# Q and K as token rows with DMA transposes, V once per token, one-bank PSUM tiles and a new written-out order in an adaLN block with dilated local attention and an MLP

## Chip, cores and metric

The kernel runs on one core of a Trainium2 chip. The metric is the device time in microseconds (us) of one execution; the median of several runs is given. A profiled execution has its own time, and the working below is made against that one.

## What is computed

One transformer block on 2048 tokens of width 448, in bf16. A conditioning vector `c` gives six modulation vectors (`sa, ca, ga, sb, cb, gb`). The first half is attention over a window of 8 keys at distance 2 (a token sees itself and the tokens 2, 4, ... 14 before it) with 16 heads of 28. The second half is an MLP of width 1792 with a layer norm of its own inside.

```python
mod = (_silu(c) @ w_mod).reshape(c.shape[0], 6, 1, -1)        # sa, ca, ga, sb, cb, gb
h = _layernorm(x) * (1 + ca) + sa
qkv = (h @ wqkv) ...                                          # q, k, v: 16 heads of 28
off = arange(8) * 2 ; idx = pos[:, None] - off[None, :]       # keys of a query
logits = einsum('bhsd,bhswd->bhsw', q, k[idx]) * 28 ** -0.5   # masked where idx < 0
o = einsum('bhsw,bhswd->bhsd', softmax(logits), v[idx])
x = x + ga * (o @ wo)
h = _layernorm(x) * (1 + cb) + sb
x = x + gb * (gelu(_layernorm(h) @ w1 + b1) @ w2 + b2)
```

## The kernel before

**Tiling.** Even and odd tokens never meet in the attention, so every buffer has a parity index `s` of two. A block `jb` (0 to 7) is 128 tokens of each parity, 256 in all. An attention step `i` (0 to 8) is 114 queries of each parity, two groups of 57, each with the 64 keys that it can see. A chunk `c` (0 to 3) of the MLP is two blocks, 512 tokens.

**Stages.** For a block: layer norm of `x` (`s1`, `r1`, `n1`: statistics, reciprocal root, normalising); the transposed block goes into `hT`, by TensorE and an eviction with the modulation (`tr`, `ev`, blocks 0 to 3) or by a DMA transpose with the modulation afterwards (`dT`, `sc`, blocks 4 to 7). Q and K come out of TensorE with their columns on the partitions (`qA`, `qB`: stationary `wqk`, a copy of the weights with heads padded to 32, made by `wc`; moving `hT`, 256 or 512 tokens), and one eviction by ScalarE per pair of banks (`qe`) puts them in `qT` and `kT`. V is computed for each step and not for each block, since the 64 keys of neighbouring groups overlap (`vA`, `vB`, lines 481 to 500, nine steps), and is evicted with keys on the partitions (`ve`).

An attention step is `L` (logits), `eA`, `eB` (exponential), `mA`, `mB` (mask), `AV` (sums, then the weighted values), `ln`, `rx` (reciprocal of the sum by logarithm and exponential), `mu` (division, into `qT`). Then for a block `wo` (output projection), `x1` (residual), `s2 r2 n2 h2 s3 r3 n3` (two layer norms and the modulation), `dY` (DMA transpose into `yT`). For an MLP chunk: `fA`, `fB` (seven pairs of 128 hidden columns), `ge` (gelu by ScalarE, 14), `f2` (second product, 14 matmuls for each of four groups of 128 tokens), `fo` (bias and residual) and `dS` (store).

A product with 448 inner elements is split over two row halves of TensorE that run side by side: part A is eight matmuls, part B six. Between them stands `ob`, an empty instruction on another engine's queue (line 437) that waits for part A and that part B waits for.

**What sets the order.** All instructions are written out by hand-made tables: `ORDER` is the sequence of items, and every engine gets its instructions in that sequence; `SLOTS` says which buffer each item uses. The four PSUM tiles of two banks each are `P`. SyncE (SP) issues all but one of the DMAs, in the same sequence, so a DMA behind a waiting one waits too; a DMA also waits for the eighth DMA before it. `tab` switches ScalarE between the table of exponential and logarithm and that of gelu, so the gelu of chunk 0 comes only after the steps that need the first table. `warm` are matmuls on zeros in the first microseconds.

Of the kernel before, what the change touches and what calls it, by code (L numbers as in the profile page):

```python
# [36 lines left out]
qA.0.1 ob.POOL.q.0.0 ob.ACT.q.1.2 n1.2 r1.3 qB.0.0 ob.ACT.q.0.1 qB.1.2 qe.0.0 tr.2 n1.3 qe.1.2 rowm ev.2.3 ev.2.2
ev.2.0 ev.2.1 tr.3 rowc qB.0.1 ev.3.2 ev.3.1 qA.0.2 ev.3.0 ev.3.3 s1.6 qA.1.1 ob.SP.q.0.2 qe.0.1 qB.0.2 ob.SP.q.1.1
qA.2.2 qe.0.2 dR s1.5 r1.6 qB.1.1 ob.SP.q.2.2 L.0 qe.1.1 s1.4 r1.5 qB.2.2 eA.0 dB qA.2.1 eB.0 mA.0 r1.4 qA.1.0 s1.7
ob.SP.q.2.1 qe.2.2 qB.2.1 ob.SP.q.1.0 qB.1.0 qe.2.1 qA.2.0 mB.0 r1.7 n1.4 dR2 qe.1.0 AV.0 ob.POOL.q.2.0 n1.5 dT.4  # L40
n1.6 qB.2.0 ln.0 qA.1.3 rx.0 dT.6 b1T ob.DVE.q.1.3 b1c qB.1.3 qe.2.0 mu.0 vA.1 dT.5 qe.1.3 vA.2 ob.POOL.v.1 wos vB.1
dW1.0.1 ob.ACT.v.2 n1.7 dW1.0.0 vB.2 ve.1 sc.4 L.1 dT.7 ve.2 qA.2.3 w2s.5 eA.1 rowf vA.3 ob.SP.q.2.3 eB.1 mA.1
qB.2.3 ob.SP.v.3 mB.1 vB.3 qe.2.3 sc.5 AV.1 ve.3 w2s.2 qA.3.3 sc.6 ln.1 qA.3.1 rx.1 ob.SP.q.3.3 sc.7 qB.3.3
ob.SP.q.3.1 mu.1 qB.3.1 qe.3.3 qA.4.3 w2s.0 qe.3.1 w2s.4 L.2 ob.SP.q.4.3 w2s.3 qB.4.3 eA.2 w2s.1 qA.4.0 w2s.6 qe.4.3
mA.2 wo.0 ob.SP.q.4.0 eB.2 mB.2 qB.4.0 x1.0 AV.2 qe.4.0 s2.0 xp.0 qA.3.2 ln.2 qA.4.2 rx.2 ob.SP.q.3.2 r2.0 qB.3.2
ob.ACT.q.4.2 mu.2 qB.4.2 qe.3.2 n2.0 L.3 qe.4.2 h2.0 wo.1 eA.3 s3.0 eB.3 qA.4.1 r3.0 qA.3.0 ob.ACT.q.4.1 n3.0 qB.4.1
ob.ACT.q.3.0 qB.3.0 mA.3 dY.0 qe.4.1 x1.1 vA.4 qe.3.0 vA.5 s2.1 ob.SP.v.4 xp.1 vB.4 ob.SP.v.5 L.4 ve.4 vB.5 mB.3
r2.1 eA.4 ve.5 mA.4 L.5 n2.1 eB.4 h2.1 eA.5 AV.3 mB.4 eB.5 vA.6 mA.5 ln.3 mB.5 ob.SP.v.6 s3.1 vB.6 rx.3 AV.4 ve.6
mu.3 r3.1 ln.4 vA.7 n3.1 rx.4 wo.2 ob.POOL.v.7 dY.1 mu.4 vB.7 x1.2 AV.5 ve.7 s2.2 xp.2 wo.3 ln.5 rx.5 fA.0.0 x1.3
tab.1 r2.2 fA.0.1 ob.SP.f.0.0 s2.3 fA.0.2 ob.SP.f.0.1 n2.2 r2.3 fB.0.1 ob.SP.f.0.2 mu.5 fB.0.2 ge.0.3 fB.0.0 ge.0.2  # L50
n2.3 fA.0.3 ge.0.4 h2.3 ge.0.0 fA.0.4 ob.SP.f.0.3 h2.2 ge.0.5 fB.0.3 ge.0.1 ob.SP.f.0.4 s3.3 fA.0.5 ge.0.7 ge.0.6
# [690 lines left out]
```

## Time and profile before

| | |
|---|---|
| median of 3 runs | 182.56 us (181.6 to 184.72) |
| profiled execution, span | 182.2 us |
| TensorE busy | 170.8 us (94% of the span), 2538 matmuls |
| VectorE, ScalarE, GpSimd busy | 112.5 us (62%), 105.0 us (58%), 43.3 us (24%) |
| mean granted TensorE clock | 0.958 of full speed |
| HBM read, written | 10.04 MB, 1.95 MB |

The profile shows the span from the first to the last instruction; no other time of that execution is recorded, so the span stands for it, and it lies 0.4 us below the median of the runs. Busy time of TensorE is the time in which a matmul was in the array or in its queue, so a stall behind a queued matmul can hide in it, and a half-speed clock makes the same matmuls look twice as busy. The granted clock is given for each stretch as a share of full speed.

### The profile page before, as it was taken

The page shows a single profiled execution, that of the slowest core. Times are in us where ns is not written, and L with a number is a line of the kernel's source. Part 1 is how long each engine was busy: PE and PEld are TensorE (multiplying, and loading weights), DVE is VectorE, ACT ScalarE, POOL GpSimd, SP SyncE. Part 2 cuts the span into 40 slices and gives each one's busy share as a digit, 9 for nine tenths or more (in the row PEclk, how much of TensorE's full clock was granted, in tenths as well). Part 3 has the DMA queues.
Part 4 walks back from the last instruction along what each step waited for, and adds up shares of the span by engine and source line. Part 5 has one row for each costly group of instructions (what it writes and reads, how often), then busy time and mean ns, then how long its engine had stood idle before and what let it go on. Part 6 is the DMA issues. An engine that isn't in the chain of part 4 may idle for free.

```text
span 182.2 us, 5815 instructions
## 1 busy us (share of the span) xinstructions
PE 170.8 (94%) x2538; PEld 86.3 (47%) x2539; DVE 112.5 (62%) x264; ACT 105.0 (58%) x145; POOL 43.3 (24%) x77
## 2 busy tenths in 40 slices
PE   7999679979999979999999999999999999999990
PEld 2556335634444453444454554554544554454550
DVE  5858757599969789589788604785970772002022
ACT  3177619777967497487884879650887000585000
POOL 7404062000050442062402500224520224400000
PEclk9969969999999995899999999999999999999998
DMA  5999994997000300300080130013103004100111
GB/s 150 321 393 302 375 312 101 117 255 153 4 4 2 61 4 4 63 0 5 0 105 14 56 58 4 4 24 84 54 4 58 0 0 108 54 0 0 54 50 50
DMA packets 21455, 15.51 MB, mean 85 GB/s; under 512 B 13301, under 2 KB 20982, under 8 KB 21430
## 3 DMA queue, kind: packets, MB, share of 16 engines
q1 hardware_dynamic: 21428, 15.14, 32.1%
q8 instruction: 20, 0.33, 0.8%
q14 instruction: 5, 0.04, 0.1%
q10 hardware_dynamic: 2, 0.00, 0.0%
HBM read 10.04 MB, written 1.95 MB: 66 GB/s over the span
## 4 chain that ended last, share of the span: by engine, by line
PE 74%; DMA 8%; DVE 7%; ACT 4%; issue 2%; SPq 1%; POOL 1%; DVEq 0%
PE P L660 21%; PE P L419 18%; PE P L428 13%; PE P L588 7%; PE P L489 7%; DMA rowd<-zt 3%; DMA bc<-rowd 3%; DMA yT<-in_w_mod_dram 2%; PE P L563 2%; DVE st L348 2%; PE P L522 1%; PE P L554 1%; PE P L261 1%; PE P L292 1%; ACT et L527 1%
## 5 line engine op out<-in xcount | busy, mean ns | idle before, releaser
L653 ACT ACTIVATE hm<-P,b1c 128x512 bf16<-128x512 f32 x56 | 34.1, 691 | 22.4 <-PE P L428 22.3
L660 PE MATMUL P<-w2s,hm 128*128 128x448 bf16 x224 | 43.4, 353 | 0.0
L660 PEld LDWEIGHTS <-hm 128*128 128x128 bf16 x224 | 21.6, 98 | 20.6 <-issue 0.8
L419 PE MATMUL P<-yT,w1s 64*128 64x512 bf16 x224 | 27.1, 376 | 0.2 <-DVE x L665 0.2
L597 POOL TENSOR_TENSOR xp<-x,gbb 128x896 f32<-128x896 bf16 x8 | 15.2, 1897 | 40.2 <-DVE x L593 27.7
L665 DVE TENSOR_TENSOR x<-P,xp 128x896 bf16<-128x896 f32 (+1 forms) x9 | 8.8, 985 | 25.8 <-PE P L660 25.7
L354 POOL TENSOR_SCALAR rs<-mv 128x2 f32<-128x2 f32 x22 | 6.7, 303 | 70.8 <-DVE mv L350 61.8
L428 PE MATMUL P<-yT,w1s 64*128 64x512 bf16 x168 | 20.9, 376 | 0.0
L348 DVE BATCH_NORM_STATS2 st<-x 128x6 f32<-128x448 bf16 x32 | 18.3, 615 | 0.9 <-DMA x<-in_A_x_dram 0.5
L489 PE MATMUL P<-wv,hT 64*64 64x448 bf16 x252 | 17.5, 397 | 0.4 <-SPq L437 0.2
L593 DVE TENSOR_TENSOR x<-P,x 128x896 bf16<-128x896 f32 x8 | 8.7, 1090 | 14.5 <-PE P L588 14.5
L419 PEld LDWEIGHTS <-w1s 64*128 64x128 bf16 x224 | 11.1, 94 | 13.0 <-issue 1.2
L527 ACT ACTIVATE et<-P 128x912 bf16<-128x912 f32 x18 | 16.1, 942 | 1.7 <-PE P L522 1.7
L419 PE MATMUL P<-hT,wqk 64*128 64x512 bf16 (+1 forms) x160 | 16.9, 347 | 0.1
L428 PE MATMUL P<-hT,wqk 64*128 64x512 bf16 (+1 forms) x120 | 13.6, 349 | 3.6 <-SPq L437 3.6
L355 POOL TENSOR_TENSOR rs<-rs,nhalf 128x2 f32<-128x2 f32 x22 | 16.0, 726 | 1.8
L568 ACT ACTIVATE rc<-P 128x912 f32<-128x912 f32 x9 | 8.5, 942 | 10.4 <-PE P L554 10.4
L540 DVE TENSOR_TENSOR et<-et,mask 128x912 bf16<-128x912 bf16 x18 | 11.3, 652 | 4.5 <-ACT et L527 4.4
L588 PE MATMUL P<-wo,qT 128*128 128x448 bf16 x64 | 13.5, 353 | 0.1
L428 PEld LDWEIGHTS <-w1s 64*128 64x128 bf16 x168 | 8.8, 94 | 9.4
L578 DVE TENSOR_TENSOR qT<-P,rc 128x456 bf16<-128x456 f32 x18 | 10.5, 624 | 2.9 <-ACT rc L573 2.9
L509 ACT CAST vs<-P 128x896 bf16<-128x896 f32 x9 | 8.1, 907 | 6.2 <-PE P L489 6.2
(79 smaller groups left out, 187.2 us busy)
## 6 DMA issues: line engine op xcount, KB each, us to landing
w1s<-in_B_w_dram SPq DMA_DIRECT2D x4, 448.0 KB, 11.7
w2s<-in_B_w_dram SPq DMA_DIRECT2D x2, 784.0 KB, 15.6
out_dram<-x SPq DMA_DIRECT2D x7, 224.0 KB, 2.3
hm<-in_w_mod_dram SPq DMA_DIRECT2D x1, 1344.0 KB
hm<-in_A_wqkv_dram SPq DMA_DIRECT2D x4, 224.0 KB, 5.1
x<-in_A_x_dram SPq DMA_DIRECT2D x1, 896.0 KB
yT<-in_w_mod_dram SPq DMA_DIRECT2D x3, 224.0 KB, 4.1
x<-in_A_x_dram SPq DMA_DIRECT2D x2, 224.0 KB
```

The lines of the kernel that those rows point to most:

```text
L348: nc.vector.bn_stats(out=self.st[:, b + s, :], in_=src[:, s, :])
L355: nc.gpsimd.tensor_tensor(out=r, in0=r, in1=self.nhalf[:], op=ALU.pow)
L419: mm = self.nc.tensor.matmul(outs[t], lhsT=lhs(t, r, kt), rhs=rhs(t, r, kt), start=(kt == 0), stop=False)
L428: mm = self.nc.tensor.matmul(outs[o], lhsT=lhs(o, r, kt), rhs=rhs(o, r, kt), start=False, stop=(n == 2))
L489: mm = self.nc.tensor.matmul(t[64 * s:64 * s + 64, o, 0:D], lhsT=self.hT[r, s, kt, k0:k0 + NK], rhs=self.wv[r, kt, :], start=(part == 0 an ...
L527: self.nc.scalar.activation(out=self.et[:, self.sl(f"e{i}"), 2 * h:2 * h + 2, :], in_=self.ps(f"L{'AB'[h]}{i}")[:, :, 0:8 * NQ], func=ACT.Exp,
L540: self.nc.vector.tensor_tensor(out=e, in0=e, in1=m, op=ALU.mult)
L578: self.nc.vector.tensor_tensor(out=self.qT[:, s, :, c0:c0 + SW], in0=self.ps(f"O{i}")[:, s, 0:8 * NQ].rearrange("p (m c) -> p m c", m=4), ...
L588: self.nc.tensor.matmul(p[:, s, 0:D], lhsT=self.qT[:, s, m, c0:c0 + 128], rhs=self.wo[:, m, :], start=(m == 0), stop=(m == 3))
L597: self.nc.gpsimd.tensor_tensor(out=self.xp[:, self.sl(f"xp{jb}"), :, :], in0=self.x[:, jb, :, :], in1=self.gbb2[:].unsqueeze(1).to_broadca ...
L653: self.nc.scalar.activation(out=self.hid(c)[:, ft, :], in_=self.ps(f"F{c}.{ft // 2}")[:, ft % 2, :], func=ACT.Gelu_apprx_tanh, bias=self.b ...
L660: self.nc.tensor.matmul(p[:, s, 0:D], lhsT=h[:, ft, 128 * b:128 * b + 128], rhs=self.w2s[:, ft, :], start=(ft == 0), stop=(ft == FT - 1))
```

## The change

**Q and K.** The operands change places: `hT` (128 tokens of a block and parity) is stationary and the weights move, 448 columns of Q and 448 of K. The result has tokens on the partitions. Two evictions (`qe`, one for Q and one for K, on ScalarE `A` or VectorE `D`) write it with heads padded to 32 into `qks`, and a DMA transpose (`qT`) of 128 rows by 1024 columns brings it into `qkT`, which takes the place of `qT` and `kT`. The padded copy of the weights (`wc`) goes.

**V.** It is computed once per block, evicted as two halves (`ve`), written to DRAM (`vw`, buffer `vd` with seven rows of zeros in front) and read back for each step and parity in the overlapping form (`vr`).

**PSUM.** Eight tiles of one bank. What was one instruction on two banks becomes two on one bank each: the exponential (`ex`, four a step), `ln`, `rx`, `mu`, `x1`, `fo`.

**Order.** Blocks 2 and 3 are transposed by DMA too (`NTR = 2`). The product for the modulation is cut into four parts that follow their loads (`mod`), `modc` sums them. `ORDER` and `SLOTS` are new throughout; the engine of each eviction stands in the item.

```diff
-i.ones i.z dX.0 dC i.one warm0 i.mask dM.0 dM.1 i.id dM.2 i.maskb i.maskc dM.3 i.eps i.pad dX.1 s1.0 cT warm1 dQ.0
+i.one i.mask i.qks i.z dM.0 dC cT silu0 i.maskc dX.1.1 dX.2.2 i.wo dO.1 dM.1 silu1 silu2 i.id s1.1 warm.0.5 dX.0.1
...
-        self.P = [ps.tile([128, 2, 512], FP32, name=f"P{i}") for i in range(4)]
+        self.P = [ps.tile([128, 512], FP32, name=f"P{i}") for i in range(8)]
...
-        def lhs(o, r, kt):
-            return self.wqk[r, kt, 128 * (2 * p + o):128 * (2 * p + o) + 128]
+    def qk(self, jb, s):
+        def lhs(o, r, kt):
+            return self.hT[r, s, kt, 128 * jb:128 * jb + 128]
         def rhs(o, r, kt):
-            return self.hT[r, :, kt, c0:c0 + 128 * nj]
+            return self.wqk[r, kt, D * o:D * o + D]
...
+    def qe(self, eng, jb, s, o):
+        out = self.qks[:, self.sl(f"q{jb}_{s}"), o, :].rearrange("p (h e) -> p h e", e=32)[:, :, 0:DH]
+        self.copy(eng, out, self.ps(f"Q{jb}_{s}")[o][:, 0:D].rearrange("p (h e) -> p h e", e=DH))
+
+    def qT(self, jb, s):
+        c0 = PADL + 128 * jb
+        src = self.qks[:, self.sl(f"q{jb}_{s}"), :, :].rearrange("p o n -> p (o n)")
+        self.nc.sync.dma_start_transpose(out=self.qkT[:, s, :, c0:c0 + 128], in_=src)
+
+    def v(self, jb):
+        def lhs(o, r, kt):
+            return self.hT[r, o, kt, 128 * jb:128 * jb + 128]
+
+        def rhs(o, r, kt):
+            return self.wv[r, kt, :]
...
+    def ve(self, eng, jb, s):
+        self.copy(eng, self.vst[:, self.sl(f"vw{jb}"), s, :], self.ps(f"V{jb}")[s][:, 0:D])
+
+    def vw(self, jb):
+        a = WIN - 1 + 128 * jb
+        self.nc.sync.dma_start(out=self.vd[:, a:a + 128, :].rearrange("s r d -> r s d"),
+                               in_=self.vst[:, self.sl(f"vw{jb}"), :, :])
+
+    def vr(self, i, s):
+        src = self.vd[s, SW * i:SW * i + NK, :]
+        src = bass.AP(src.tensor, src.offset, [list(src.ap[0]), [NQ * D, 2], [1, D]])
+        self.nc.sync.dma_start(out=self.vs[64 * s:64 * s + 64, self.sl(f"v{i}"), :, 0:D], in_=src)
...
-    def exp_(self, i, h):
-        self.nc.scalar.activation(out=self.et[:, self.sl(f"e{i}"), 2 * h:2 * h + 2, :],
-                                  in_=self.ps(f"L{'AB'[h]}{i}")[:, :, 0:8 * NQ], func=ACT.Exp,
-                                  scale=float(DH) ** -0.5)
+    def ex(self, i, r):
+        self.nc.scalar.activation(out=self.et[:, self.sl(f"e{i}"), r, :], in_=self.ps(f"L{i}")[r][:, 0:8 * NQ],
+                                  func=ACT.Exp, scale=float(DH) ** -0.5)
```

How the queues stand before and after is shown at two places.

SyncE's queue between the first DMA transpose and the read of the modulation rows (`bc<-rowd`), before. `hT<-yz` is `dT`, `w1s` are MLP weights, `rowd` and `bc` carry the modulation rows:

```order
L314 DMA rowd<-zt 128x448
L191 DMA b1r<-in_B_b_dram 14x128
L192 DMA b2bc<-in_B_b_dram 128x448
L318 DMA bc<-rowd 128x4x448
L405 DMA_TRANSPOSE hT<-yz 128x8x128 x3
L157 DMA w1s<-in_B_w_dram 128x2x896 x2
L405 DMA_TRANSPOSE hT<-yz 128x8x128
L629 DMA_TRANSPOSE yT<-yz 128x8x128 x4
```

And after, the twelve rows up to that read and past it (`qkT<-qks` is `qT`, `vd<-vst` is `vw`, `vs<-vd` is `vr`):

```order
L332 DMA rowd<-rows 128x448
L512 DMA vs<-vd 64x2x448
L505 DMA vd<-vst 128x2x448
L512 DMA vs<-vd 64x2x448 x2
L484 DMA_TRANSPOSE qkT<-qks 128x8x128
L505 DMA vd<-vst 128x2x448
L206 DMA wo<-in_A_wo_dram 28x4x448
L512 DMA vs<-vd 64x2x448
L336 DMA bc<-rowd 128x4x448
L206 DMA wo<-in_A_wo_dram 28x4x448 x2
L484 DMA_TRANSPOSE qkT<-qks 128x8x128
L512 DMA vs<-vd 64x2x448
```

What stood in a queue of 28 DMAs now stands in one of 95, with 30 transposes instead of 12, and the reads of V and the transposes of Q and K alternate with the loads.

VectorE's queue before the transposed block 1 of the MLP input (`yz<-h2t`, the `n3` whose `dY` opens chunk 0), before: from the residual of block 1 to that instruction.

```order
L593 TENSOR_TENSOR x<-P_66,x 128x896
L348 BN_STATS st<-x 128x6 x2
L350 BN_AGGR mv_108<-st 128x2 x2
L540 TENSOR_TENSOR et<-et,mask 128x912 x2
L358 TENSOR_SCALAR zz<-x,mv_108,rs_111 128x448 x2
L612 TENSOR_TENSOR h2t<-zz,g_86 128x896
L613 TENSOR_TENSOR h2t<-h2t,bc 128x896
L540 TENSOR_TENSOR et<-et,mask 128x912 x3
L348 BN_STATS st<-h2t 128x6 x2
L350 BN_AGGR mv_109<-st 128x2 x2
L578 TENSOR_TENSOR qT<-P_63,rc 128x4x114 x2
L358 TENSOR_SCALAR yz<-h2t,mv_109,rs_112 128x512 x2
```

The same piece after, from the statistics of block 1 on (`qks<-P` is a `qe` on VectorE, `qkT<-P,rc` a half of `mu`):

```order
L369 BN_AGGR mv_113<-st 128x2 x2
L537 TENSOR_TENSOR et<-et,mask 128x912 x3
L377 TENSOR_SCALAR zz<-x,mv_113,rs_116 128x448 x2
L603 TENSOR_TENSOR h2t<-zz,g_89 128x896
L604 TENSOR_TENSOR h2t<-h2t,bc 128x896
L473 CAST qks<-P_64 128x16x28
L367 BN_STATS st<-h2t 128x6 x2
L369 BN_AGGR mv_114<-st 128x2 x2
L568 TENSOR_TENSOR qkT<-P_68,rc 128x4x114
L377 TENSOR_SCALAR yz<-h2t,mv_114,rs_117 128x512 x2
L568 TENSOR_TENSOR qkT<-P_67,rc 128x4x114
L377 TENSOR_SCALAR yz<-h2t,mv_114,rs_117 128x512 x2
```

Here `n3` of block 0 has moved down to stand just ahead of that of block 1, an eviction of Q or K has come in, and the division of a step is in two halves.

More of the change, by code (lines that the diff above doesn't have):

```diff
@@ L37 @@
[L37 to L51, printed above, removed]
@@ L288, in mod, with silu2 @@
+    def silu2(self):
+        self.nc.vector.tensor_copy(out=self.silub[:], in_=self.silu[:].unsqueeze(2).to_broadcast([128, 4, 32]))
+    def mod(self, kt):
+        p, r = self.ps("mod"), slice(0, min(128, D - 128 * kt))
         for v in range(2):
             for j in range(4):
-                for kt in range(4):
-                    r = slice(0, min(128, D - 128 * kt))
-                    self.nc.tensor.matmul(p[:, 1, 4 * v + j:4 * v + j + 1],
-                                          lhsT=self.wm1[r, kt, v * D + KO[j]:v * D + KO[j] + 128],
-                                          rhs=self.silu[r, kt:kt + 1], start=(kt == 0), stop=(kt == 3))
+                n = 8 * kt + 4 * v + j
+                self.nc.tensor.matmul(p[:, n:n + 1], lhsT=self.wm1[r, kt, v * D + KO[j]:v * D + KO[j] + 128],
+                                      rhs=self.silu[r, kt:kt + 1], start=True, stop=True)
@@ L478, in qe @@
             self.nc.scalar.copy(out=out, in_=src)
-    def v_(self, i, part):
-        t = self.ps(f"V{i}")
-        for n in range(4 if part == 0 else 3):
-            for row in range(2):
-                o = row if part == 0 else 1 - row
-                kt = n if part == 0 else REST[o][n]
-                k0 = PADL + SW * i + NQ * o - (WIN - 1)
-                r = slice(64 * row, 64 * row + 64)
-                for s in range(2):
-                    mm = self.nc.tensor.matmul(t[64 * s:64 * s + 64, o, 0:D], lhsT=self.hT[r, s, kt, k0:k0 + NK],
-                                               rhs=self.wv[r, kt, :], start=(part == 0 and n == 0),
-                                               stop=(part == 1 and n == 2), tile_position=(64 * row, 64 * s))
-                    if part == 1 and n == 0:
-                        self.tc.add_manual_dep(mm.ins, self.half[f"V{i}"], SYNC, reason="half")
-        if part == 0:
-            self.half[f"V{i}"] = mm
@@ new lines, in qT, with vA @@
+    def qT(self, jb, s):
[7 more added lines that the diff above has]
+            return self.wv[r, kt, :]
+        return [p[:, 0:D] for p in self.ps(f"V{jb}")], lhs, rhs
+    def vA(self, jb):
+        self.first(f"V{jb}", *self.v(jb))
```

355 lines of the change are left out of this document (167 added, 188 removed).

## The prediction

> **What bounds the kernel now.** I read the page first, then two stretches of the span: from the first to the last matmul of the MLP, and the attention stage ahead of it. Columns are length, busy time of TensorE, weight loads, VectorE, ScalarE and GpSimd, granted clock, share of the DMA engines, GB/s.
>
> ```profile
> PE 170.8 (94%) x2538; PEld 86.3 (47%) x2539; DVE 112.5 (62%) x264; ACT 105.0 (58%) x145; POOL 43.3 (24%) x77
> ...
> 79.50:178.10 98.60, 98.29 (x1085) 48.96 (x1084) 51.03 (x106) 52.61 (x75) 21.82 (x29) 1.00 0.15 34
> ...
> 30.00:80.00 50.00, 47.22 (x1151) 23.34 (x1149) 40.90 (x96) 37.38 (x44) 11.52 (x15) 0.93 0.34 62
> ```
>
> TensorE is the bound: from 79.5 it is busy 98.29 of 98.60 us. Between 30 and 80 it is busy 47.22 of 50, with VectorE at 40.90 and ScalarE at 37.38, so neither follows far behind. Next the chain that ended last (start, length, what), for the price of each product at full speed.
>
> ```profile
> 46.19 0.86 PE P L419 x8
> 47.05 0.63 PE P L522 x64
> 54.38 1.29 PE P L428 x12
> 77.05 0.32 PE P L554 x8
> 77.37 0.55 PE P L563 x64
> 77.92 1.62 PE P L588 x8
> 79.54 2.70 PE P L419 x24
> 111.46 0.88 PE P L489 x16
> 112.97 0.69 PE P L489 x12
> 134.60 2.59 PE P L419 x24
> 137.19 1.94 PE P L428 x18
> 140.76 13.24 PE P L660 x70
> 164.73 13.36 PE P L660 x70
> 178.21 0.62 DVE x L665
> ```
>
> The MLP opens at 79.54 (x24 are three parts A of chunk 0), and from there the end is a sum. One of 28 pairs takes (2.59 + 1.94) / 3 = 1.51, in all 42.3; 224 second products at 13.24 / 70 make 42.4; four `wo` at 1.62 make 6.5; three `L` 1.9; three `AV` at 0.87 make 2.6; the last V 0.88 + 0.69 = 1.6. That is 97.3, and TensorE took 164.73 + 13.36 - 79.54 = 98.55, so it lost 1.25. The tail from 178.09 to 182.2 is 4.1 (last `fo`, its store). So **end = start of the MLP + TensorE's work behind it + 1.25 + 4.1**, and the question is what the change does to these two.
>
> **The change part by part.** *TensorE, Q and K.* A product of 512 columns costs 0.86 + 1.29 / 2 = 1.505. Before there are 12 of these and 8 of 256 columns, at half: 24.1. After there are 16 of 448; scaled by columns 1.32 each, 21.1. Bounds: this, and no gain if weight loads set the pace (1.505, 24.1). I take the scaled one, as weight loads are busy 47% of the span. *V*: nine at 1.57 before, 14.1; eight at 1.32 after, 10.5.
>
> ```profile
> L390 PE MATMUL P<-ident,zz 128*128 128x128 bf16 x32 | 2.9, 244 | 0.0
> ```
>
> 16 of these 32 transposes go, 1.4. Together TensorE loses 8.0 us of work, all of it ahead of the MLP but for the last V (1.6) and two `L`, which now stand in front. Behind the first MLP product remain 42.3 + 42.4 + 6.5 + 0.6 + 2.6 = 94.4.
>
> *The other engines.* They get more. Forms with busy time and mean of one:
>
> ```profile
> L411 DVE TENSOR_SCALAR hT<-hT,mcol 128x256 bf16<-128x256 bf16 x16 | 4.4, 341 | 0.2 <-DMA hT<-yz 0.2
> L400 ACT ACTIVATE hT<-P,mcol 128x256 bf16<-128x256 bf16 x8 | 4.4, 567 | 3.1 <-DVE hT L397 2.8 <-PE P L390 0.3
> L527 ACT ACTIVATE et<-P 128x912 bf16<-128x912 f32 x18 | 16.1, 942 | 1.7 <-PE P L522 1.7
> L311 ACT CAST zt<-P 128x448 bf16<-128x448 f32 x1 | 0.5, 522 | 0.0
> L540 DVE TENSOR_TENSOR et<-et,mask 128x912 bf16<-128x912 bf16 x18 | 11.3, 652 | 4.5 <-ACT et L527 4.4
> L578 DVE TENSOR_TENSOR qT<-P,rc 128x456 bf16<-128x456 f32 x18 | 10.5, 624 | 2.9 <-ACT rc L573 2.9
> L348 DVE BATCH_NORM_STATS2 st<-h2t 128x6 f32<-128x448 bf16 x16 | 9.2, 614 | 0.1
> L350 DVE BATCH_NORM_AGGREGATE mv<-st 128x2 f32<-128x6 f32 x48 | 7.2, 174 | 0.0
> L358 DVE TENSOR_SCALAR zz<-x,mv,rs 128x448 bf16<-128x448 bf16 x24 | 8.5, 395 | 3.3 <-POOL rs L355 3.2
> L613 DVE TENSOR_TENSOR h2t<-h2t,bc 128x896 bf16<-128x896 bf16 x8 | 5.0, 625 | 0.3
> L665 DVE TENSOR_TENSOR x<-P,xp 128x448 bf16<-128x448 f32 x2 | 1.2, 620 | 4.2 <-PE P L660 4.2
> ```
>
> A one-bank exponential, logarithm or eviction on ScalarE lies between half of 16.1 / 18 (0.45) and 0.52; I take 0.50. An eviction with 28 of every 32 columns on VectorE is shown nowhere: between 8.5 / 24 = 0.35 and 0.60 (1.2 / 2, the same 448 columns out of PSUM); I take 0.60, the nearer row. The modulation of a transposed block is 0.28 on VectorE, 0.55 on ScalarE.
>
> Now the stretch from the first logits to the MLP, after. Logits of step 0 follow six Q-K products and three V, 11.9 us, behind a first product at about 12 to 13, and one stretch at half speed adds 1.7: 26, about where they are before. The first mask should come where it did:
>
> ```profile
> 28.64 0.63 DVE L540 TENSOR_TENSOR et<-et,mask 128x912 bf16<-128x912 bf16 x1 [3.33 <-ACT et L527]
> ```
>
> From that mask to `n3` of block 1 VectorE has to do, counted in its new order: 11 masks (6.9), 10 modulations (2.8), 7 evictions (4.2), 8 halves of `mu` (4.7), 4 halves of `x1` (2.4), 4 statistics at 2 x 0.575 + 2 x 0.15 (5.8), 8 normalisings at 0.36 (2.9) and two more for blocks 6 and 7 (1.4 in all), 4 modulations of the MLP input (2.5), `wos` and small ones (1.7): **35 us**. ScalarE in the same stretch: 28 exponentials, 21 evictions and 16 others of one bank (32.5) and 6 modulations (3.3), **36**. TensorE: 10 Q-K, 5 V, 8 `L`, 6 `AV`, 4 `wo` and the modulation rows, 13.2 + 6.6 + 5.0 + 5.2 + 6.5 + 1.0 = **37.5**. So in this stage three engines are level, where TensorE alone was the bound, and the way runs through all three at each step.
>
> Then the queue of SyncE, which was idle for most of the span. Durations are shortest, median and longest in ns, for the two lines that transpose and the one that stores:
>
> ```profile
> L405 SPq DMA_TRANSPOSE hT<-yz x4: 1302/1546/2950, 31.8 to 38.8; - x4
> ...
> L629 SPq DMA_TRANSPOSE yT<-yz x8: 1232/1232/1977, 61.0 to 149.8; - x8
> ...
> DMA to landing us min/median/max: 3.1/3.1/3.3
> ...
> L670 SPq DMA_DIRECT2D out_dram<-x x9: 332/332/517, 99.9 to 179.4; - x9
> ...
> DMA to landing us min/median/max: 1.7/1.9/2.7
> ```
>
> Ahead of the `dY` that opens the MLP it has 17 transposes and 26 other DMAs from the first logits on: 17 x 1.30 + 26 x 0.4 = 32.5 us, which fits. Behind a waiting transpose stand the write and the reads of V, and `AV` waits for those. I cost a `qT` at nothing, since between a block's Q-K product and the logits of it stand one or two products of other blocks (1.3 to 4 us) and its landing is 3.1; without that cover each costs up to 3.1. V's way through DRAM costs two landings of 1.7 to 2.7 (6 at most where bulk loads stand ahead); before there was none. Its cover is longer, `vA.1` to `AV.1` is some 15 us, so nothing again.
>
> *When the MLP starts.* 28.6 + 35 / share + 3.1. With VectorE's share of 30 to 80 (40.90 / 50 = 0.82) this is 74.4; with a share of 0.98 it is 67.4.
>
> ```profile
> 40.00:50.00 10.00, 9.32 (x208) 4.46 (x209) 9.82 (x26) 7.81 (x9) 0.00 (x0) 1.00 0.46 106
> ```
>
> Such a share is reached for 10 us only (this row, 9.82). I take **73.5**, near the first: with three engines level each hand-over costs somebody time. End: 73.5 + 94.4 + 1.25 + 4.1 = 173.3 against the span of 182.2; the median of the runs stood 0.4 above the span, so **173.6 us**.
>
> *The clock.* Part of the time lost today is TensorE at half speed:
>
> ```profile
> 65.00:66.00 1.00, 0.63 (x47) 0.37 (x39) 0.28 (x1) 1.00 (x2) 0.76 (x2) 1.00 0.00 0
> 66.00:67.00 1.00, 0.41 (x46) 0.39 (x30) 0.97 (x4) 1.00 (x2) 0.00 (x0) 1.00 0.07 16
> 67.00:68.00 1.00, 0.63 (x59) 0.55 (x59) 0.97 (x2) 1.00 (x3) 0.00 (x0) 0.93 0.00 0
> 73.00:74.00 1.00, 1.00 (x25) 0.54 (x16) 0.07 (x1) 0.97 (x2) 0.00 (x0) 0.50 0.00 0
> ```
>
> After three us at a busy share near 0.56 the clock falls (0.93 is its mean over the last of them) and it still is 0.50 at 73 to 74: six us at half speed, three of them lost. After, TensorE has 37.5 us of work in 73.5 - 26 = 47.5, a share of 0.79, so there will be such stretches; its slack takes some of the loss, which is why I don't go to the low end. The Trainium skill, "TensorE: Matmul & The Clock Gate", section "Why this matters for your kernels", asks for no idle gaps over about 3 us; by that rule the stage would have no half speed at all, and the start of the MLP would be nearer 67.4 than 73.5. The trace does not bear that out: no gap in these rows is as long as 1 us.
>
> **The rivals.**
>
> *Nothing gained.* TensorE stays the bound ahead of the MLP because its holes keep the clock at half. Four further stretches of 3.4 us at half speed, 1.7 each, put the MLP at 73.5 + 6.8 = 80.3 and the end at 180.4. For: the rows above. Against: half-speed time costs only where TensorE is waited for.
>
> *Slower: SyncE's queue.* The second of the three transposes in a row held the queue 2.95 (the longest in its row), with a bulk load in flight. If that is the rule after, 17 x 2.95 + 10 = 60 puts `dY` of block 1 at 86, the MLP at 89 and the end at 189. It is slower than 2% from a mean hold of 2.8. For: the stage now loads weights, V and transposes in one queue. Against: the median of the eight later ones is 1.232, the first and third in a row took 1.30 or little more.
>
> *More gained.* The three engines interleave as tightly as between 40 and 50; MLP at 67.4, end at 167.5.
>
> *The MLP stage does not stay full.* With the work ahead of it gone sooner, a chunk could wait for its `dY`; VectorE has 51.03 and ScalarE 52.61 of 98.6 there, which leaves room, and I give it no case of its own.
>
> **How the numbers follow.** Forecast (170 to 178.5) 0.48; more gained (below 170) 0.18; nothing gained (179 to 186) 0.20; slower by the queue 0.14. The range leaves out little of the second and most of the last: 167.5, the tight interleaving, to 183, past the half-speed case. About 2% can be told from no change: faster than 178.9 is 0.48 + 0.18 = 0.66, within 0.20, slower 0.14.
>
> **What would show it.** Right: the first MLP matmul near 73.5; about 95.7 us from it to the last matmul; Q-K pairs at 1.32; VectorE and ScalarE above 0.8 between 30 and 70, TensorE near 0.8. Wrong: the MLP at 80 with rows of clock 0.50 ahead of it; transposes holding SyncE over 2 us; `L` or `AV` released by a DMA; TensorE idle by more than 2 us behind the first MLP product, which would undo the second half of the sum.

## The result and the profile after

| | before | after |
|---|---|---|
| median of 4 runs each, same chip | 182.88 us (181.6 to 184.72) | 190.19 us (189.01 to 193.88) |
| profiled span | 182.2 us | 187.8 us |
| ratio after / before | | 1.036 [1.027, 1.045] |

The changed kernel is slower by 3.6%. The forecast was 173.6 us, in a range of 167.5 to 183. Most kernels of the experiments that leave work out ran once; the four executions of the changed kernel have spans of 187.3 to 192.2 us, so 2 us between two single spans say little.

First the page of the changed kernel: busy time of the engines, the DMA queue that SyncE feeds (packets, MB, share of 16 engines), and the chain that ended last, by engine.

```profile
PE 163.7 (87%) x2327; PEld 79.5 (42%) x2328; DVE 118.8 (63%) x279; ACT 102.7 (55%) x192; POOL 43.3 (23%) x73
...
q1 hardware_dynamic: 45220, 23.76, 57.0%
...
PE 54%; DMA 23%; ACT 8%; DVE 8%; POOL 3%; issue 2%; SPq 1%; DVEq 0%; POOLq 0%; ACTq 0%
```

TensorE did lose work: 170.8 us of busy time became 163.7. But it is no longer the bound: transfers are now nearly a quarter of the chain. The two stretches that answer to those of before, from the first to the last matmul of the MLP and the 50 us of attention:

```profile
84.50:184.20 99.70, 97.47 (x928) 46.88 (x928) 56.68 (x125) 49.97 (x80) 26.81 (x30) 0.98 0.25 60
...
30.00:80.00 50.00, 38.94 (x1003) 19.23 (x999) 35.54 (x82) 36.13 (x78) 4.09 (x8) 0.97 1.02 187
```

Between 30 and 80 no engine is near full: TensorE 38.94 of 50 us (47.22 before), VectorE 35.54 (40.90), ScalarE 36.13. The granted clock is 0.97, better than the 0.93 of before, so half-speed stretches are not what was lost. The share of the 16 DMA engines is 1.02 where it was 0.34 (the times of all packets are added up for it, so it can pass 1). Next, the first MLP matmul in the timeline (start, length), and the waits that belong to it:

```profile
84.50 2.77 PE L436 MATMUL P<-yT,w1s 64*128 64x512 bf16 x24 [0.25 <-DVE x L583]
```

```profile
PE P L526 <- DMA qkT<-qks: 8.8, 6, 3.7
...
DVE wo L346 <- DMA wo<-in_A_wo_dram: 5.2, 1, 5.2
PE P L436 <- DMA yT<-yz: 2.0, 1, 2.0
```

The MLP opens at 84.5, against 79.5 before and 73.5 in the forecast: 11 us too late. The logits (L526) waited six times for a transpose of Q and K, 8.8 us in all, and the transposes land late (DMA issues, median us to landing; the `dY` of before took 3.1):

```profile
qkT<-qks SPq DMA_TRANSPOSE x16, 4.9
```

The wait invites a first reading: DMA engines full, so that transposes land late and the logits wait. The experiments showed that this reading is largely wrong. What to look at is SyncE's queue, as the timeline shows it. Before, in the stretch up to the read of the modulation rows (`bc<-rowd`, L318) and past it:

```profile
21.69 2.03 SPq L187 DMA_DIRECT2D wo<-in_A_wo_dram  x4
24.00 0.37 SPq L314 DMA_DIRECT2D rowd<-zt  x1
26.46 0.33 SPq L191 DMA_DIRECT2D b1r<-in_B_b_dram  x1
27.32 0.36 SPq L192 DMA_DIRECT2D b2bc<-in_B_b_dram  x1
30.27 0.39 SPq L318 DMA_DIRECT2D bc<-rowd  x1
31.75 5.75 SPq L405 DMA_TRANSPOSE hT<-yz  x3
```

And after:

```profile
28.88 1.44 SPq L424 DMA_TRANSPOSE hT<-yz  x1
30.41 0.53 SPq L505 DMA_DIRECT2D vd<-vst  x1
31.05 3.23 SPq L484 DMA_TRANSPOSE qkT<-qks  x2
34.38 1.79 SPq L424 DMA_TRANSPOSE hT<-yz  x1
36.26 0.54 SPq L332 DMA_DIRECT2D rowd<-rows  x1
36.90 0.65 SPq L512 DMA_DIRECT2D vs<-vd  x1
37.60 0.58 SPq L505 DMA_DIRECT2D vd<-vst  x1
38.24 1.25 SPq L512 DMA_DIRECT2D vs<-vd  x2
39.60 1.26 SPq L484 DMA_TRANSPOSE qkT<-qks  x1
40.97 1.34 SPq L505 DMA_DIRECT2D vd<-vst  x1
42.37 0.46 SPq L206 DMA_DIRECT2D wo<-in_A_wo_dram  x1
42.88 0.59 SPq L512 DMA_DIRECT2D vs<-vd  x1
43.52 0.60 SPq L336 DMA_DIRECT2D bc<-rowd  x1
```

The length of a row is the time for which the instruction held the queue; a row of several (x2, x3) also holds the gaps between them. In the second list each row starts about 0.1 us after the end of the one ahead of it: SyncE hardly rests. Added up over its single DMAs, without the gaps, SyncE is held for 49.5 of the 58 us from 26 to 84 (12.7 before), and for 30.1 of the 33 us from 20 to 53. The modulation rows are read at 43.52 instead of 30.27, the last three loads of the output weights go out at 42 to 45 (all four at 22 to 24 before), and VectorE stands 5.2 us for these weights with the division of step 0 behind it in its queue.

### The profile page after: what moved, and what is told of

Its sections match the earlier page's. It is cut to its first block, busy times and chain, and to the rows that moved or that the text cites. A ratio compares the mean times of both kernels' runs of the same rounds, so it can differ in the third digit from the quotient of the medians.

```text
span 187.8 us, 5537 instructions
## 1 busy us (share of the span) xinstructions
PE 163.7 (87%) x2327; PEld 79.5 (42%) x2328; DVE 118.8 (63%) x279; ACT 102.7 (55%) x192; POOL 43.3 (23%) x73
## 4 chain that ended last, share of the span: by engine, by line
PE 54%; DMA 23%; ACT 8%; DVE 8%; POOL 3%; issue 2%; SPq 1%; DVEq 0%; POOLq 0%; ACTq 0%
PE P L650 23%; PE P L436 13%; DMA qkT<-qks 12%; PE P L445 9%; PE P L578 5%; DMA hT<-yz 5%; DMA yT<-yz 3%; ACT hT L416 2%; DMA yT<-in_w_mod_dram 2%; DVE st L367 2%; DMA vs<-vd 2%; ACT qks L475 2%; ACT vst L475 1%; ACT et L531 1%; PE P L526 1%
## 5 line engine op out<-in xcount | busy, mean ns | idle before, releaser
L436 PE MATMUL P<-yT,w1s 64*128 64x512 bf16 x224 | 28.5, 393 | 2.2 <-DMA yT<-yz 2.0
L654 DVE TENSOR_TENSOR x<-P,xp 128x448 bf16<-128x448 f32 x16 | 9.5, 619 | 31.1 <-PE P L650 31.1
L436 PE MATMUL P<-hm,hT 64*128 64x448 bf16 x192 | 22.0, 351 | 2.0 <-ACT vst L475 1.1
L445 PE MATMUL P<-yT,w1s 64*128 64x512 bf16 x168 | 20.8, 376 | 0.2
L531 ACT ACTIVATE et<-P 128x456 bf16<-128x456 f32 x36 | 17.2, 559 | 6.6 <-PE P L526 6.5
L445 PE MATMUL P<-hm,hT 64*128 64x448 bf16 x144 | 16.7, 350 | 0.7 <-SPq L453 0.3
L578 PE MATMUL P<-wo,qkT 128*128 128x448 bf16 x64 | 15.0, 382 | 0.0
L526 PE MATMUL P<-qkT 28*64 28x57 bf16 x576 | 7.0, 200 | 8.8 <-DMA qkT<-qks 8.8
L475 ACT CAST qks<-P 128x448 bf16<-128x448 f32 x22 | 11.0, 547 | 5.5 <-PE P L445 4.3
L436 PEld LDWEIGHTS <-hT 64*128 64x128 bf16 x192 | 8.7, 94 | 11.1 <-issue 3.3
L583 DVE TENSOR_TENSOR x<-P,x 128x448 bf16<-128x448 f32 x16 | 9.5, 617 | 3.7 <-PE P L578 3.1
L568 DVE TENSOR_TENSOR qkT<-P,rc 128x456 bf16<-128x456 f32 x18 | 10.8, 623 | 1.5 <-ACT rc L564 1.4
```

What stands on the lines that cost most here:

```text
L436: mm = self.nc.tensor.matmul(outs[t], lhsT=lhs(t, r, kt), rhs=rhs(t, r, kt), start=(kt == 0), stop=False)
L445: mm = self.nc.tensor.matmul(outs[o], lhsT=lhs(o, r, kt), rhs=rhs(o, r, kt), start=False, stop=(n == 2))
L475: self.nc.scalar.copy(out=out, in_=src)
L531: self.nc.scalar.activation(out=self.et[:, self.sl(f"e{i}"), r, :], in_=self.ps(f"L{i}")[r][:, 0:8 * NQ], func=ACT.Exp, scale=float(DH) ** ...
L568: self.nc.vector.tensor_tensor(out=self.qkT[:, s, 0:4, c0:c0 + SW], in0=self.ps(f"O{i}")[s][:, 0:8 * NQ].rearrange("p (m c) -> p m c", m=4 ...
L578: self.nc.tensor.matmul(p[s][:, 0:D], lhsT=self.qkT[:, s, m, c0:c0 + 128], rhs=self.wo[:, m, :], start=(m == 0), stop=(m == 3))
```

## Experiments: which part of the change

**Without the hop of Q and K.**

```diff
     def qT(self, jb, s):
+        return
...
-   lhsT=self.qkT[rr, s, 4 + m, k0:k0 + NK], rhs=self.qkT[rr, s, m, q0:q0 + NQ]
+   lhsT=self.hT[rr, s, m, k0:k0 + NK],      rhs=self.hT[rr, s, m, q0:q0 + NQ]
```

> The changed kernel without the 16 transposes of Q and K: the logits read the transposed block itself and wait neither for the transposes nor for the evictions ahead of them, so the values are meaningless. The bound on what the whole hop can cost. A and B: first MLP matmul at 70 to 75 (my prediction without the hop said 73.5), span 173 to 178, and the other transposes (hT, yT) land in 3.1 to 3.5 instead of 3.5 to 4.9. C (order, one-bank tiles): first MLP matmul above 80, span 184 or more.

Measured: span 175.6, first MLP matmul and attention stretch:

```profile
74.22 2.77 PE L436 MATMUL P<-yT,w1s 64*128 64x512 bf16 x24 [0.22 <-DMA yT<-yz]
```

```profile
30.00:80.00 50.00, 44.43 (x1169) 23.59 (x1171) 42.80 (x101) 42.62 (x89) 6.76 (x12) 1.00 0.68 152
```

74.22 is near the 73.5 of my sum, and VectorE's share is 0.86 against the 0.82 that I had taken. So the sum of the engines' work fits, and order and one-bank tiles show no loss here. The lateness against this kernel, 10.3 us, hangs on the hop: the 16 transposes, and the wait for them and for the evictions ahead of them.

**Without V's trip, and without either.** `vw`, `vr` and the zeros in front are left out:

```diff
     def vw(self, jb):
+        return
     def vr(self, i, s):
+        return
```

> The changed kernel without V's way through DRAM: no writes, no reads back, the values of V are zeros that stand in the buffer from the start. A: 26 plain DMAs of 112 or 224 KB go, about 17 us of 16 engines' time out of 107, so transposes of Q and K land in about 4 instead of 4.9, and the span falls by 3 to 5, to 183 to 185. V's trip as the main cause: 8 or more, to 180 or less. B (SyncE's queue): 26 holds of 0.57 us go, which gives as much as A, but the landings of the transposes stay at 4.9.

> The changed kernel with neither the transposes of Q and K nor V's way through DRAM: the logits read the transposed block itself, V is zeros, so the values are meaningless. What order and tiles are worth alone. The two apart gave 12.2 (without the hop) and 4.9 (without V's trip) of 187.8. A: they share one resource, so together less than the sum: 172 to 175, MLP at 71 to 74. Independent costs: 170 to 171.

Without the trip: span 182.9, MLP at 78.62, transposes landing in 4.2 us. Without either: span 176.6, MLP at 73.87. V's trip costs 4.9 us of span where the transposes are there and nothing that shows (176.6 without it, 175.6 with it) where they are not. The two share something that has room for one of them. Both candidates, DMA engines and SyncE's queue, fit that.

## Experiments: what of the hop costs

**The transposes issued, and not waited for by the logits.** All as in the changed kernel, but the logits read `hT` as above.

> The changed kernel with its 16 transposes of Q and K issued as they were, with all their traffic, but the logits read the transposed block itself and so wait for none of them (the values are meaningless). It parts the two ways in which the hop can cost: its own landing in the path of the logits, or the traffic that it puts in the way of the others. With neither (an earlier run) the first MLP matmul stood at 74.2, with both at 84.5. If the landing in the path is all: 74 to 76, span 175 to 178. If the traffic is all: 82 to 85, span 185 to 188. I expect both, the landing more: 76 to 79, 178 to 181, with V's reads and the other transposes late.

```profile
86.64 4.27 PE L436 MATMUL P<-yT,w1s 64*128 64x512 bf16 x24 [3.66 <-DMA yT<-yz]
```

```profile
43.83 0.92 SPq L336 DMA_DIRECT2D bc<-rowd  x1
```

Span 189.6, the MLP at 86.64: as late as with the wait. My expectation (76 to 79) missed. The 8.8 us that the logits wait in the changed kernel are not what makes it late; when that wait is gone, others take its place, since whatever else stands in SyncE's queue is as late as before (the modulation rows again at 43.8). One kind of wait for the transposes is left in this kernel: an eviction of Q or K waits until the transpose has read its buffer, 5.1 us in two waits (1.3 in three in the changed kernel).

**Cheaper transfers in the same places.** Plain copies of the same bytes, then transposes of K alone:

```diff
-        self.nc.sync.dma_start_transpose(out=self.qkT[:, s, :, c0:c0 + 128], in_=src)
+        self.nc.sync.dma_start(out=self.qkT[:, s, :, c0:c0 + 128], in_=src)           # first kernel
+        self.nc.sync.dma_start_transpose(out=self.qkT[:, s, 4:8, c0:c0 + 128], in_=self.qks[..., 1, :])   # second
```

> The changed kernel, but the 16 transposes of Q and K become plain copies of the same bytes from the same rows to the same place (256-byte pieces); Q and K are then not transposed, so the values are meaningless and only the time is read. If the transposing traffic fills the DMA engines (A): copies land in about 2.5 us instead of 4.9, the DMA share between 30 and 80 falls from 1.02 to about 0.6, the first MLP matmul moves from 84.5 to 74 to 78 and the span from 187.8 to 177 to 181. If SyncE's queue is what binds (B): copies still stand in the same queue but hold it 0.5 instead of 1.3 us, so the hop shortens by 0.8 and the span by 3 to 6, with landings near 4.9 as before. If the order or the one-bank tiles are to blame (C): no change, 186 to 189.

> The changed kernel with K alone transposed (128 rows by 512 columns instead of 1024, half the bytes and half the pieces, the same 16 issues); the queries are read from the transposed block, so the values are meaningless. If the DMA engines' time for these bytes sets the landing: qkT lands in about 3.2 to 3.7 instead of 4.9, the first MLP matmul at 77 to 80, span 179 to 183. If each issue or landing has a fixed price whatever its size: landings stay above 4.5 and the span at 185 to 188.

DMA issues of the first (KB each, median us to landing), and the holds of the transposes in the second (shortest, median, longest ns):

```profile
qkT<-qks SPq DMA_DIRECT2D x16, 256.0 KB, 5.0
```

```profile
L484 SPq DMA_TRANSPOSE qkT<-qks x16: 1188/1230/1601, 20.7 to 72.5; - x16
```

Plain copies land no sooner (5.0 us against 4.9), so the late landing is not the transposing; they hold the queue for 0.65 us (median) instead of 1.32; span 185.4, MLP at 83.5. Half the bytes land in 3.9 us, but hold the queue nearly as long (1.23 against 1.32); span 182.9, MLP at 81.6. Neither theory had the first result right. The second, 2.9 us sooner with nearly the same holds, speaks for the traffic having some part.

**Without the loads of the first MLP weights** (1.8 MB, four DMAs):

> The changed kernel without the loads of the first MLP weights: 1.8 MB less between 45 and 84 us; the first MLP product reads another weight tile, so the values are meaningless. A (sum of DMA engine time): the loads are large pieces, some 1.8 MB at 250 to 300 GB/s or 6 to 7 us of 16 engines, so 2 to 4 us faster, 184 to 186, MLP at 80.5 to 82.5. If small packets alone are the trouble: no change, 187 to 189.

Span 188.2: nothing gained, neither from the 1.8 MB less nor from the 2.8 us less for which SyncE was held. These loads stand late in the queue, from 56 us on in the changed kernel.

## Experiments: SyncE's queue by itself

**Holds without traffic.** The kernel without the hop, with two DMAs of 16 bytes, and then with one, in the place of each transpose. They wait for the same evictions.

```diff
     def qT(self, jb, s):
+        for o in range(2):                     # range(1) in the second kernel
+            c = 8 * (4 * jb + 2 * s + o)
+            self.nc.sync.dma_start(out=self.scr[0:1, c:c + 8], in_=self.qks[0:1, self.sl(f"q{jb}_{s}"), o, 0:8])
```

> The kernel without the hop (logits read the transposed block itself and wait for nothing of Q and K, values meaningless; it had the first MLP matmul at 74.2 and a span of 175.6), with two DMAs of 16 bytes in place of each transpose. They wait for the same evictions and hold SyncE about as long (2 x 0.6 us), and move next to nothing. If SyncE's queue is the cause (B): SyncE is busy for some 50 of the 58 us from 26 to 84 again, the modulation rows are read back at 43 instead of 37, and the MLP starts at 80 to 85, span 181 to 187. If the traffic on the DMA engines is the cause (A): MLP at 74 to 77, span 175 to 178.

> The run with two 16-byte DMAs in each transpose's place had its first MLP matmul at 82.2 with SyncE busy 46.2 of the 58 us from 26 to 84; without any, 74.2 and 32.1. This is the same kernel with one such DMA in each place (logits read the transposed block itself, values meaningless): half the dose. B: SyncE busy about 38 to 40, MLP at 77 to 80, span 179 to 183. If the number of DMAs in flight or something else with a threshold were the cause: 74 to 75 or 82 as with two.

With two: the holds (ns), the attention stretch, the read of the modulation rows and the first MLP matmul.

```profile
L485 SPq DMA_DIRECT2D scr<-qks x32: 619/640/1350, 20.6 to 73.5; - x32
```

```profile
30.00:80.00 50.00, 41.84 (x1135) 21.83 (x1131) 38.01 (x88) 38.72 (x84) 5.20 (x10) 0.97 0.62 134
```

```profile
42.47 0.59 SPq L337 DMA_DIRECT2D bc<-rowd  x1
```

```profile
82.19 4.05 PE L437 MATMUL P<-yT,w1s 64*128 64x512 bf16 x24 [2.15 <-DMA yT<-yz]
```

And with one:

```profile
79.22 2.77 PE L437 MATMUL P<-yT,w1s 64*128 64x512 bf16 x24 [0.99 <-DVE st L368]
```

A DMA of 16 bytes holds SyncE for 0.64 us. The DMA engines' share stays at 0.62, below the 0.68 of the kernel without the hop, and no logits wait for these bytes; still 8.0 of the 10.3 us are back with two, 5.0 with one, and the spans are 187.1 and 182.5. The tiny DMAs bring back two things of SyncE's queue: the holds, and the places where the queue stands for an eviction. Besides, evictions stood 3.0 us for them with two and 1.2 us with one, since a buffer must be read before it is written again. The runs do not part these. SyncE's own wait for the eighth DMA before is not what came back: from 20 to 88 its list of waits names no landing, neither in the changed kernel nor with two tiny DMAs. The table sets SyncE's held time from 26 to 84 (added up over the single DMAs, so a little below the sums that the expectations quote) beside the first MLP matmul:

```
kernel                        SyncE held   MLP starts   span
without hop                      30.8         74.2      175.6
without hop, one tiny DMA        40.3         79.2      182.5
without hop, two tiny DMAs       44.6         82.2      187.1
changed kernel                   49.5         84.5      187.8
changed, logits do not wait      50.6         86.6      189.6
without V's trip                 39.8         78.6      182.9
without either                   14.3         73.9      176.6
K alone transposed               46.7         81.6      182.9
plain copies                     45.6         83.5      185.4
without first MLP weights        46.7         84.7      188.2
```

From the first row to the fourth, each us of SyncE's time costs about half a us at the MLP: (82.2 - 74.2) / (44.6 - 30.8) = 0.58, (84.5 - 74.2) / (49.5 - 30.8) = 0.55. Below the first row no cost shows: without either, SyncE is held 16.5 us less than without the hop, and the MLP starts 0.3 us sooner. So here the queue begins to cost somewhere between 31 and 40 of 58 us. That fits V's trip, which is free without the transposes and dear beside them. The last two rows lie 1.2 and 1.8 above a line of 0.55 and K alone 1.3 below it, so the held time is not all: where in the queue it goes, or the bytes, may count too.

## Experiments: relieving SyncE with nothing left out

**V's trip on GpSimd's queue; ten DMAs, then eight of the transposes, on ScalarE's.**

```diff
-        self.nc.sync.dma_start(out=self.vs[64 * s:64 * s + 64, ...    # vw, vr: GpSimd
+        self.nc.gpsimd.dma_start(out=self.vs[64 * s:64 * s + 64, ...
...
-        self.nc.sync.dma_start(out=self.wo[32 * r:32 * r + DH, ...    # dO, dW1, dNx, dR: ScalarE
+        self.nc.scalar.dma_start(out=self.wo[32 * r:32 * r + DH, ...
...
-        self.nc.sync.dma_start_transpose(out=self.qkT[...             # 8 of 16 qT: ScalarE
+        self.nc.scalar.dma_start_transpose(out=self.qkT[...
```

> The changed kernel with V's writes and reads issued on GpSimd's queue instead of SyncE's; nothing is left out, the bytes are the same. A (DMA engines full): no gain, 186 to 190, transposes of Q and K still at 4.9. B (SyncE's in-order queue delays the transposes behind V's waiting DMAs): several us faster, 180 to 184, first MLP matmul at 78 to 81. GpSimd also does evictions' work elsewhere (reciprocal roots), so a loss of 1 to 3 is possible under A.

> The changed kernel with ten DMAs off SyncE's queue and on ScalarE's: the loads of the output weights and the first MLP weights, the last piece of the modulation weights, and the write of the modulation rows. The same traffic, nothing left out. B: SyncE loses 5 to 6 of its 52 us, ScalarE (busy 43 of 58) gets them; the modulation rows are read back at 40 to 42 instead of 43.5, MLP at 80 to 83, time 185 to 189 against 190.2. A: no change, 189 to 192.

> The changed kernel with 8 of the 16 transposes of Q and K (those of block halves that ScalarE evicts last) issued on ScalarE's queue. The same traffic, nothing left out. B: SyncE loses 10 to 13 of 52 us, but ScalarE gets 10.4 on top of 43 of 58, so the bound moves there: MLP at 79 to 84, time 184 to 190. A: no change, 189 to 192. If ScalarE's holds are worth more than SyncE's: slower than 192.

The first came to a span of 193.1 with the MLP at 90.9. GpSimd's in-order queue now stands where SyncE's did:

```profile
POOL vs L512 <- DMA vd<-vst: 9.9, 2, 5.1
```

The second came to 193.53 us, 1.061 [1.052, 1.069] of before, with the MLP at 88.9. SyncE lost ten DMAs and was held nearly as long, 47.5 us: the holds that remained grew, those of the `hT` transposes to a median of 2.09 us (1.66 in the changed kernel, 1.33 without the hop):

```profile
L429 SPq DMA_TRANSPOSE hT<-yz x6: 1240/2094/3227, 16.5 to 50.6; - x6
```

The third came to 216.02 us, 1.184 [1.171, 1.196]. Its profile is of an execution of 223.66 us, the longest of five. SyncE was down to 24.6 us held from 26 to 84, but the MLP opens at 115.4: TensorE waited 11.0 us for `ob` items in ScalarE's queue, where the transposes now stand, and SyncE's `hT` transposes waited 8.2 us for landings of `qkT`:

```profile
PE P L445 <- ACTq L453: 11.0, 2, 5.7
```

**One transpose for both parities** (eight of 2048 columns in place of sixteen of 1024), and with that the weight loads on GpSimd's queue:

```diff
-        self.nc.sync.dma_start_transpose(out=self.qkT[:, s, :, c0:c0 + 128], in_=src)
+        out = self.qkT[:, :, :, c0:c0 + 128].rearrange("p s m n -> p (s m) n")
+        self.nc.sync.dma_start_transpose(out=out, in_=src)
```

> The changed kernel with one transpose of 128 rows by 2048 columns for both parities of a block in place of two of 1024: 8 issues instead of 16, the same bytes and pieces; each waits for both parities' evictions. Nothing is left out. B: a hold hardly depends on size (1.23 us for 512 columns, 1.32 for 1024), so SyncE is rid of some 10 of its 52 us, and the kernel is 3 to 8 us faster than the changed one: 182 to 187. A: the traffic is the same, so 188 to 192, or worse for the wait for the second parity.

> As the run before with one transpose for both parities, and besides the loads of the output weights, the MLP weights and the later modulation weights are issued on GpSimd's queue. Nothing is left out. B: SyncE loses another 5 to 7 us of holds, so 1 to 4 us faster than with the pairs alone: 179 to 185. A: no change against the pairs alone, within 1 us, or slower by the extra instructions on GpSimd.

195.13 us, 1.065 [1.056, 1.074], and 203.96, 1.116 [1.106, 1.125]. The premise was wrong: a hold is the same for 512 and 1024 columns, but not for 2048. Besides, with two buffers for both parities the evictions wait for the transposes:

```profile
L444 SPq DMA_TRANSPOSE qkT<-qks x8: 1785/3092/5070, 22.8 to 81.4; - x8
```

```profile
ACT qks L434 <- DMA qkT<-qks: 15.2, 3, 6.8
```

These two say nothing on the cause, since a new wait came in with the edit. None of the five gained: with each relief of SyncE came waits in another engine's queue, waits for a buffer, or longer holds.

## Experiments: undoing parts

**Q and K as before in the changed kernel**, with 256 tokens a product, and then for blocks 2 to 7 alone with 512:

```diff
-            return self.hT[r, s, kt, 128 * jb:128 * jb + 128]          # stationary
+            return self.wqk[r, kt, 128 * (2 * p + o):128 * (2 * p + o) + 128]
-            return self.wqk[r, kt, D * o:D * o + D]                    # moving
+            return self.hT[r, :, kt, 128 * jb:128 * jb + 128]
```

> The changed kernel with the change of Q and K undone: padded weights stationary, columns on the partitions out of TensorE, evictions straight into the buffer that the logits read, no transposes. V once per token, one-bank tiles and the new order stay; 8 copies of the weights come back. Nothing is left out. The run without the hop put the MLP at 74.2 and the span at 175.6; TensorE pays 3 us more for Q and K here and a wait between the two products of a bank pair. A (DMA engines full, by Q and K first of all): first MLP matmul at 76 to 80, 177 to 182 in all, so as fast as before or up to 3 percent faster. If the order needs the transposes' timing, or the extra instructions of one-bank tiles bind: 184 or more. The rest of V's DMA trips remains: share of the DMA engines near 0.7 between 30 and 80.

> The changed kernel with Q and K of blocks 2 to 7 undone: columns on the partitions out of TensorE, 512 tokens a product as in the kernel before (an earlier run with 256 tokens a product made TensorE the bound), evicted into the buffer that the logits read; 8 copies of the weights come back, 12 of 16 transposes go. Blocks 0 and 1 keep rows and transposes. Nothing is left out. TensorE pays 12 x (1.505 - 1.32) = 2.2 us more than after. A (the hop is what cost): first MLP matmul at 75 to 79, time 176 to 181, 1 to 4 percent faster than before. If order and tiles need what they were laid out for: 183 to 188.

The first: 189.10 us, 1.031 [1.023, 1.040], with the MLP at 85.0. SyncE is held for 24.9 us only and the clock is 1.00; TensorE is the busiest engine, and it waited 3.9 us for the copied weights:

```profile
30.00:80.00 50.00, 44.87 (x1270) 29.68 (x1265) 37.35 (x85) 40.60 (x86) 6.09 (x12) 1.00 0.58 129
```

```profile
L392 PE MATMUL P<-hT,wqk 64*128 64x256 bf16 x128 | 9.9, 274 | 4.9 <-ACT wqk L457 3.9 <-ACT vst L457 0.5 <-ACT hT L372 0.3
```

The 274 ns are the length of one record, and these overlap. The eight matmuls of a part A start within 0.34 us here and within 0.65 us with 512 columns in the kernel before, so half the columns take half the time. The second ran from 187.42 to 194.29 us (before: 180.27 to 185.24), too scattered for a size, though every run is longer than every one of before. Its profile has the MLP at 87.9 with SyncE held 27.6 us and a clock of 0.91 from 30 to 80. So a light queue alone does not make this order fast once Q and K are made the other way. Why is not shown; the order was laid out for the new way, and neither is a clean undoing.

**V's change alone, in the kernel before**, with the read behind the write, and then with the empty instructions of SyncE on GpSimd and the reads behind the logits:

```diff
+        self.nc.sync.dma_start(out=self.vd[:, a:a + 128, :]..., in_=self.vst[:, jb % 2])
+        self.nc.sync.dma_start(out=self.vs[64 * s:64 * s + 64, self.sl(f"v{i}"), :, 0:D], in_=src)
...
-ob.SP.
+ob.POOL.
```

> The kernel before with the change of V alone: V once per block, evicted by ScalarE, written to DRAM and read back for each step on SyncE's queue; order, tiles, Q and K as before (the V of step 8 goes). Nothing is left out. TensorE loses 14.1 - 10.5 = 3.6 us, all ahead of the MLP but for step 8's 1.6 behind its start. If V's trip is hidden where the DMA engines have room (share 0.34 there before): 3 to 5 faster, 177.5 to 180. If the trip is a cost in itself (two landings of 2.7 before each AV, with no cover in this order): AV waits for the reads, 2 to 8 slower than before, 185 to 191.

> The kernel before with the change of V alone, as in the run that came to 213.85, but with the empty instructions of SyncE's queue moved to GpSimd's and each read of V back from DRAM moved behind the logits of its step. If SyncE's queue, standing at a write or read of V while TensorE's halves wait for an empty instruction behind it, was the loss there: most of the 30 us go, 180 to 188. If the trip through DRAM is late by itself in this order (vA.i to AV.i leaves less than two landings): 190 to 205, with AV released by a DMA.

213.85 us, 1.156 [1.143, 1.169], and 193.82, 1.069 [1.051, 1.087]. Waits of the first and of the second:

```profile
PE P L430 <- SPq L439: 30.2, 4, 11.9
```

```profile
PE P L535 <- DMA vs<-vd: 12.4, 6, 5.2
```

In the first TensorE stood 30 us for four empty instructions that stood in SyncE's queue behind a read of V, which waited for its write. With those moved, what stays is the trip itself: the weighted values wait 12.4 us for it.

## Why the prediction was wrong, by its steps

- **The step that failed: "17 x 1.30 + 26 x 0.4 = 32.5 us, which fits".** It set a total against the length of the stage, and its terms were too small. Holds in the changed kernel (shortest, median, longest ns):

```profile
L484 SPq DMA_TRANSPOSE qkT<-qks x16: 1245/1316/2400, 20.7 to 76.0; - x16
...
L424 SPq DMA_TRANSPOSE hT<-yz x6: 1336/1658/3034, 14.8 to 51.6; - x6
...
L512 SPq DMA_DIRECT2D vs<-vd x18: 573/596/1177, 36.9 to 111.1; - x18
```

  1.30 was right as a median and left out the long holds; 0.4, taken from a store, was 0.6. The 17 transposes ahead of that `dY` held the queue for 26.8 us (1.58 on average) and the 26 others for 16.8 (0.64): 43.6 us in place of 32.5. The larger error is "which fits". 43.6 us still fit into the 51 us from the first of these DMAs to the `dY`, and the MLP came 11.0 us late: here what the queue carried came late well before it was full, and a DMA that waited in it delayed all behind it.
- **The rival "slower: SyncE's queue" named the right engine and the wrong price.** It was to decide from a mean hold of 2.8 us, with the MLP at 89. It decided at a mean of 1.58, with the MLP at 84.5. I had let it cost nothing until the total passed the stage's length; the tiny DMAs show half a us for each us held, from somewhere above 31 of 58 us on.
- **A `qT` at nothing: wrong, and not for the reason given.** The cover of 1.3 to 4 us against a landing of 3.1 (4.9 it became) was the wrong thing to weigh: with no logits waiting for the landing the kernel was as late.
- **V's trip at nothing: wrong in this company.** 4.9 us of span beside the transposes, none that shows without them.
- **35 us of VectorE's work at a share of 0.82 from 28.6, landing 3.1, MLP at 73.5: right** without the hop (74.2, share 0.86). With it the share was 35.54 / 50 = 0.71.
- **TensorE's prices: right.** A part A and a part B at full speed, from the chain of the kernel with neither hop nor trip, make 1.33 against the 1.32 that was scaled:

```profile
19.49 0.76 PE P L437 x8
20.25 0.57 PE P L446 x6
```

- **"94.4 + 1.25" behind the first MLP matmul: too small.** From 84.50 to the last matmul at 184.2 it took 99.7, where 95.65 was forecast (97.8 without the hop). Chunk 1 waited 1.96 us for a `dY` and then ran at half speed (the timeline's row, and the clock of that stretch), the case that I had named and given no chance:

```profile
101.19 3.48 PE L436 MATMUL P<-yT,w1s 64*128 64x512 bf16 x16 [1.96 <-DMA yT<-yz]
```

```profile
101.00:104.70 3.70, 3.51 (x18) 1.49 (x20) 3.70 (x9) 2.22 (x3) 0.93 (x2) 0.54 0.04 7
```

- **From span to run: too small, 0.4.** The profiled execution of the changed kernel has a span of 187.8 us and a run time of 189.51, 1.7 more. The kernel before shows the like (180.6 and 182.47 us in one execution), so its profiled execution, with 182.2, was probably longer than its median run.
- **The clock.** It was 0.97 between 30 and 80, so "nothing gained" by half speed did not happen. In the last row above it fell to 0.54 behind a wait of 1.96 us. The Trainium skill, "TensorE: Matmul & The Clock Gate", "Why this matters for your kernels", asks for no gaps over about 3 us; this trace, like the one of before, does not bear that limit out.

What stays open: whether the full DMA engines add anything beside the queue. Two tiny DMAs in each place reach 82.2 and the real transposes 84.5; the rest, 2.3 us, can be traffic or the longer holds, and no run parts the two. The holds are not independent of what else is under way: those of the `hT` transposes have a median of 1.33 us without the hop, 1.58 with two tiny DMAs and 1.66 in the changed kernel. With plain copies the MLP starts 1.3 us later than with two tiny DMAs, at about the same held time (45.6 and 44.6). These are single executions. No kernel with right values became faster when SyncE was relieved, so what a lighter queue alone would give was not seen. What the new order is worth with Q, K and V made as before was not tried: the undoings brought new waits.

## What to carry to other kernels

Count an in-order DMA queue as an engine: number of DMAs times the hold of each kind, taken from rows of the same kind under load, against the stretch in which they must go, and expect lateness long before it is full: here none showed at 31 of 58 us held, and 5 us at 40. A wait for a DMA's landing names the last link only; before you blame the landing, take the wait away and leave the traffic, then put the issues back without the traffic. Moving DMAs to an engine that computes puts their holds and waits ahead of that engine's own work.

## What the runs showed of the hardware

- A DMA of 16 bytes held SyncE for 0.64 us, a read of 112 KB for 0.60: the hold is not a matter of bytes at this size.
- A transpose of 128 rows held it for 1.23 us with 512 columns, 1.32 with 1024 and 3.09 with 2048 (medians).
- A plain copy of 256 KB in pieces of 256 bytes landed in 5.0 us, the transpose of the same bytes in 4.9.
- The records of matmuls on half the rows are 274 ns long with 256 columns and 351 with 448, but overlap: the eight of a part A start within 0.34, 0.58 and 0.65 us with 256, 448 and 512 columns.
- V's trip, which took SyncE from 14 to 31 us held of 58, moved the start of the MLP by 0.3 us; two tiny DMAs in the place of each transpose, from 31 to 45, moved it by 8.0.
